# Sum of a state-space convolution and a gated linear unit: the first loads in halves, the transposes of the next blocks moved, and a new hand-written order of all steps

## The chip, the core and the metric

The kernel runs on one core of one Trainium2 chip. The metric is device time in microseconds (us) of one execution; three executions of the kernel before took 239.5, 239.64 and 239.75 us, so its median is 239.64 us. Lower is better. The engines are named as in the profile: PE is the matrix engine (TensorE; PEld are its weight loads), DVE the vector engine, ACT the scalar engine, POOL is GpSimd, and SP the sync engine, which only issues transfers (DMAs).

## What is computed

`x` is 2048 rows of 640, bf16. Its layernorm `xn` goes through two branches, and the result is the sum of both and of `x`:

```
xn = layernorm(x)                                  # x = A_q
k_shift = 4-tap causal filter of k along the rows  # taps shift_k, one set per column
kv  = k_shift * v
y   = causal convolution of kv with ssm_k along the rows (by FFT of 4096) + kv * ssm_D
A   = xn * y
B   = (sigmoid(xn @ w_gate) * (xn @ w_up)) @ w_down      # 640 -> 1728 -> 640
out = x + A + B
```

## The kernel before, in words

**Tiling.** The 2048 rows lie as 128 partitions times 16 blocks. The gated branch goes in four passes t = 0 to 3 of four blocks (512 rows) each; the convolution in five chunks c = 0 to 4 of 128 columns, each by a two-stage transform in matmuls whose intermediate results go out to DRAM and come back in another layout.

**The start** (L469 to L508). SP and ACT issue the loads of `x` blocks 0 to 3 and of the first columns of both weights (`load_w`, L171; `w[:, :, 0:256]` and `[256:512]`). PE runs 15 matmuls on a zeroed tile (`busy`), while DVE takes the layernorm of blocks 0 to 3 (`ln_stats`, `ln_aggr`, `ln_var`, `ln_xn`, with a power on POOL). For each block i of the first pass, `turn(i)` transposes `xn` on PE (`xn_mm`, L234) and copies the result on ACT (`xn_ev` through L223) to `xnT`; then four `quarter`s (L248) of five 128x128 matmuls each make the block's share of gate and up for the first two column groups fc = 0 and 1. In the kernel before, `turn(1)` stands behind the first two quarters of block 0, `turn(2)` and `turn(3)` behind the first and second pair of block 1.

**Everything else** is a list of steps, written to one program order per engine by a long string, `ORDER`. A letter takes the next step of its chain. Each engine works its own steps off in that order, and waits where data or a buffer is not there yet. The letters:

- `g`: a product of the gated branch on PE: a gate or up product of five 512-column matmuls (L257), at the end of a pass the one for the last 64 columns of both (`both_mm`, L278), or seven matmuls of the down projection (`down_mm`, L296).
- `s`: the sigmoid on ACT (L266, L284). `u`: the product with up on DVE (`up_ev` L272, `both_mul` L287), or the addition of the down result to `x` (L301).
- `k`: one of 16 DVE operations per chunk that make `kv` (`kv_op`, L329 to L338; the first of a chunk writes `acc` at L329). `H`, `D`: the turn of the filter on DVE (L315) and an addition on POOL. `t`, `Z`: the taps, on ACT or, for chunk 0, on POOL.
- `a`, `A`, `w`: first transform stage on PE (L355, L357), its copy on ACT, its write to DRAM (`wr1`, SP). `r`, `b`, `B`, `p`: read back (`rd2`, SP), second stage on PE (L388), copies on ACT, the two products on DVE (L401, L403). `c`, `C`, `W`: first inverse stage on PE (L417), copies on ACT, write to DRAM (`wr2`). `R`, `d`, `q`: read back (`rdb`), second inverse stage on PE (L456), and on DVE the product with `xn` (L461) and the addition to `x` (L466).
- `l`, `P`, `e`, `E`: layernorm on DVE and POOL, transposes on PE and copies on ACT for the passes 1 to 3.
- `m`, `n`, `h`, `K`, `V`, `T`, `o`: loads and stores, all issued by SP, in order.

**Buffers that tie the engines.** Products of the gated branch, transposes of passes 1 to 3 and `psb` share four PSUM tiles (`psG`, given out in rotation): the fifth tile needs the first one's reader to be done. For the last transpose of a pass (the fourth `e`), the tile needed is that of `both_mm`, which `both_mul` on DVE (L287) reads. The transform stages share two tiles (`psC`), read by ACT.

Of the kernel before, what the change touches and what calls it, by code (L numbers as in the profile page):

```python
# [19 lines left out]
P = 128  # L20
# [37 lines left out]
def kernel(  # L58
# [14 lines left out]
    nc = tc.nc  # L73
    xr = A_q.flatten_outer_dims().rearrange("(p b) d -> p b d", b=NB)
# [9 lines left out]
    S1d = nc.inline_tensor(s1bits, name="tabS1")  # L84
    TBd = nc.inline_tensor(tbbits, name="tabTB")
    SMd = nc.inline_tensor(smbits, name="tabSM")
# [11 lines left out]
    S1t = res.tile([P, NB, 2, P], U16, name="S1t")  # L98
    TBt = res.tile([P, 2, NB, P], U16, name="TBt")
    SMt = res.tile([P, 3, 32], U16, name="SMt")  # L100
# [4 lines left out]
    x = res.tile([P, NB, DM], BF16, name="x")  # L105
# [15 lines left out]
    sync = nc.sync  # L121
# [49 lines left out]
    def load_w(eng, lo, hi, u):  # L171
        if u == 0:
            eng.dma_start(w[:, :, lo:hi], wgr[:, :, lo:hi])
            return
        h = min(hi, 13 * P)
        eng.dma_start(w[:, :, UP + lo:UP + h], wur[:, :, lo:h])
        if hi == FF:
            eng.dma_start(w[:, :, FF:UP], wur[:, :, h:FF])
# [51 lines left out]
    def xn_mm(g, i):  # L230
        pool, tag = (psG, "g") if g else (psC, "c")
        xts[i] = pt = pool.tile([P, NC, P], BF16, name="pt", tag=tag)
        for c in range(NC):
            nc.tensor.transpose(pt[:, c, :], xn[:, 4 * g + i, c * P:(c + 1) * P], ident[:])  # L234

    def xn_ev(g, i, copy=act_copy):
        copy(out=xnT[:, i, :, :], in_=xts[i][:, :, :])
# [4 lines left out]
    def quarter(u, fc, i):  # L242

        if i == 0:
            pgs[u, fc] = psG.tile([P, 512], F32, name=("pg", "pu")[u], tag="g")
        o = u * UP + fc * P
        for c in range(NC):
            nc.tensor.matmul(pgs[u, fc][:, i * P:(i + 1) * P], lhsT=w[:, c, o:o + P], rhs=xnT[:, i, c, :],  # L248
                             start=(c == 0), stop=(c == NC - 1))
# [216 lines left out]
        nc.vector.tensor_tensor(xs, xs, chunks[c]["yx", m][:, :, :], ALU.add)  # L466


    sync.dma_start(x[:, 0, :], xr[:, 0, :])  # L469
    nc.scalar.dma_start(x[:, 1, :], xr[:, 1, :])  # L470
    nc.scalar.dma_start(x[:, 2:4, :], xr[:, 2:4, :])
    for u in range(2):
        load_w((sync, nc.scalar)[u], 0, 256, u)
    for u in range(2):
        load_w(sync, 256, 512, u)

# [7 lines left out]
    def turn(i):  # L484
        xn_mm(0, i)
        xn_ev(0, i)
# [13 lines left out]
    for i in range(4):  # L500
        for fc in range(2):
            for u in range(2):
                quarter(u, fc, i)
            if (i, fc) in ((0, 0), (1, 0), (1, 1)):
                turn(1 + i + fc)
    for fc in range(2):
        gate_ev(0, fc)
        up_ev(0, fc)  # L508
# [4 lines left out]
    def step(k, fn, *args):  # L513
        chains[k].append((fn, args))
# [16 lines left out]
    def hs(c):  # L531
        return [(load_h, c)]

    def ks(c):
        return [(load_halo, c), (load_k, c, 0, 8), (load_k, c, 8, NB)]

    def vs(c):
        return [(load_v, c, 0, 8), (load_v, c, 8, NB)]

    for k in ((load_w, sync, 512, 768, 0),  # L540
              (load_w, sync, 512, 768, 1),
              (load_taps, 0),
              (sync.dma_start, SMt[:], SMd.ap()),
              (load_w, sync, 768, 1024, 0),
              (load_w, sync, 768, 1024, 1),
              (load_w, sync, 1024, 1280, 0),
              (load_w, sync, 1024, 1280, 1),
              (load_wd, sync, 0, 7),
              *ks(0),
              (load_w, sync, 1280, FF, 0),  # L550
              (load_w, sync, 1280, FF, 1),
              *hs(0),
              *vs(0),
              (load_wd, sync, 7, NFC),
              (sync.dma_start, S1t[:], S1d.ap()),
              *hs(1),
              (load_x, sync, 1),
              *ks(1),
              *vs(1)):
        step("m", *k)  # L560
    for k in ((load_x, sync, 2), (load_x, sync, 3), (sync.dma_start, TBt[:], TBd.ap())):
        step("n", *k)
    step("Z", taps, 0)

# [54 lines left out]
        step("o", store, b, b + 1, 0, DM)  # L619

    ORDER = """
    mmmmmmmmmmZgmgsmgumgsmgugsgugsmgugskgkugkskgumkgsmkgumkgsmTguHgsHDgumgskkgukgskmgukgskgumkgkmgmutmkm
    auTaAHgAHDagAwlhauaAlglaglguwlgkPkgAulgAllleKeuKwEekaEekaEgkEVVHAgAHDgwughkgkugkskguKrrkaskaAgkAkguw
    gkskgutkgTskgkKuKaksaAKkgAkaugAwkaksaAkgkwakAgVuAVHasgwHDAauhgAkgkskwbugBrkgBkktbgpBrTkgBpsapsaAuguA
    apKgKswAkaugAkaKkwsakgVHAVgAuDHgswkcugCkgkskCgnuWakaAkgAkgukwbguBrlgBlgulbgBrlgBuglkPpgnulgllleenuEe
    kbEeprgEEgptkBgupBgkaauAgpAkapgswAkaugAkawksaAgkAkguwlcsglCgClbusgrlBWgBkugslpPkaauAgllAlglspwbgBruR
    kgBkscpguCpgCksWbkgBrugBkksbpgBrudBpdgsRqpcqgCqugCqpsWbgBrukgBspbgBrupdBadqsaApRgqAqapgwAqauseeEueaE
    egEEgAgAwaudAdqgwqRqcugCqgCguWbgBrgBugpbpdBrdqgBuqgqpcqgCupgCguWbgBrgBugpspRbgBrugBspcguCpgsCguWbsdr
    BdqgRBqqguqbpsgrBpgBugpspcgCugCsWbguBrdBgqspbqgBupgBspgucpsdCgRqRCqguWbsgBgBugpspgudsdqcqgCqoqdCudqg
    WqqgsqgugoguRRguggugguogodudqogqqogqdoudqogqqogqguogoouo  # L630
    """
    left = {k: iter(v) for k, v in chains.items()}
    for k in "".join(ORDER.split()):
# [33 lines left out]
```

## Time and profile before

| what | value |
|---|---|
| median of three executions | 239.64 us (239.5 to 239.75) |
| the profiled execution's own time | 239.41 us |
| its span, first to last instruction | 237.6 us |
| granted PE clock | 1.00 of full speed over the span |
| ACT busy | 141.2 us |
| HBM read, written | 36.12 MB, 18.35 MB |
| transfers, share of 16 DMA engines (hardware queue of SP) | 80.8% |
| down products, L296 | 448 matmuls, 64.3 us busy |
| gate and up products, L257 | 500 matmuls, 124.3 us busy |

The span is what the trace covers; 1.8 us of the profiled execution's time lie outside it. Durations below come from this one execution. A row such as "L257 ... x250 | 62.2, 379" gives the busy time of a group in us and the mean length of one instruction in ns; matmuls overlap, so the distance from one start to the next (the pitch) is shorter: five 512-column matmuls start 1.08 us before the next five. An "idle before" names what ended the wait.

### The profile page before, as it was taken

What the parts mean: (1) busy time and instruction counts of PE and PEld (TensorE: products, weight loads), DVE (VectorE), ACT (ScalarE), POOL (GpSimd) and SP (SyncE); (2) the same over time, 40 slices, a digit from 0 to 9 for tenths busy, and PEclk for the clock granted to TensorE, in tenths of its full rate; (3) what the DMA queues carried; (4) which work ended last, traced back from release to release, by engine and by line L of the source; (5) the groups of instructions that cost most, each with busy time, mean ns of one, the idle gap of its engine ahead of it and who ended that gap; (6) DMA issues with size and microseconds to landing.
All of it is one profiled execution on the core that took longest, in us unless ns stands there. A gap on an engine that the chain in (4) does not pass through costs nothing.

```text
span 237.6 us, 5553 instructions
## 1 busy us (share of the span) xinstructions
PE 231.4 (97%) x2265; PEld 135.1 (57%) x2265; DVE 190.3 (80%) x350; ACT 141.2 (59%) x178; POOL 11.2 (5%) x24
## 2 busy tenths in 40 slices
PE   8799999999999999999999999999999999999994
PEld 2564445878556455667754434577664434456782
DVE  3633889999999999999999999865585695968372
ACT  2342331728559897864888887997558858764000
POOL 4210000020000000002001000000000000000000
PEclk9999999999999999999999999999999999999999
DMA  7999999889998999999444888975939795285674
GB/s 212 292 314 233 259 322 298 183 249 284 253 311 243 253 295 297 284 267 319 148 183 152 234 230 258 227 228 203 241 109 222 186 281 123 89 238 144 196 237 134
DMA packets 88975, 54.82 MB, mean 231 GB/s; under 512 B 47670, under 2 KB 83062, under 8 KB 88694
## 3 DMA queue, kind: packets, MB, share of 16 engines
q1 hardware_dynamic: 88006, 53.66, 80.8%
q10 hardware_dynamic: 944, 0.82, 1.1%
q8 instruction: 17, 0.28, 0.5%
q14 instruction: 8, 0.07, 0.1%
HBM read 36.12 MB, written 18.35 MB: 229 GB/s over the span
## 4 chain that ended last, share of the span: by engine, by line
PE 95%; DMA 3%; ACT 0%; DVE 0%; ACTq 0%; issue 0%
PE pd L296 26%; PE pg L257 23%; PE pu L257 23%; PE psb L456 4%; PE ps L357 4%; PE ps L355 4%; PE ps L388 3%; DMA w<-in_B_w_up_dram 3%; PE psa L417 2%; PE pg L278 2%; PE pt L234 2%; PE pu L248 1%; PE pg L248 1%; ACT xnT L223 0%; DVE x L301 0%; ACT L119 0%
## 5 line engine op out<-in xcount | busy, mean ns | idle before, releaser
L257 PEld LDWEIGHTS <-w 128*128 128x128 bf16 x500 | 46.5, 98 | 54.3 <-issue 5.3
L296 PE MATMUL pd<-wd,hT 128*128 128x320 bf16 x448 | 64.3, 299 | 0.0
L257 PE MATMUL pg<-xnT,w 128*128 128x512 bf16 x250 | 62.2, 379 | 0.0
L257 PE MATMUL pu<-xnT,w 128*128 128x512 bf16 x250 | 62.1, 379 | 0.0
L296 PEld LDWEIGHTS <-hT 128*128 128x128 bf16 x448 | 42.8, 98 | 17.8 <-issue 1.7
L266 ACT ACTIVATE sig<-pg 128x512 bf16<-128x512 f32 x52 | 31.3, 605 | 30.1 <-PE pg L257 28.2
L272 DVE TENSOR_TENSOR hT<-sig,pu 128x512 bf16<-128x512 bf16 x52 | 35.2, 679 | 14.7 <-PE pu L257 9.3
L223 ACT CAST t<-ps 128x1024 bf16<-128x1024 f32 x40 | 39.1, 1023 | 11.4 <-DMA d<-t 6.3
L223 ACT CAST xz<-ps 128x1024 bf16<-128x1024 f32 x40 | 38.6, 1018 | 10.6 <-PE ps L388 10.5
L301 DVE TENSOR_TENSOR x<-pd,x 128x320 bf16<-128x320 f32 x32 | 15.4, 480 | 15.8 <-PE pd L296 15.7
L403 DVE TENSOR_TENSOR xz<-xz 128x2048 bf16<-128x2048 bf16 x20 | 24.4, 1220 | 0.2
L357 PE MATMUL ps<-kvh,S1t 128*128 128x128 bf16 x160 | 21.2, 219 | 0.0
L335 DVE TENSOR_TENSOR acc<-acc,tmp 128x1024 bf16<-128x1024 bf16 x30 | 20.7, 689 | 0.7
L355 PE MATMUL ps<-kvh,S1t 128*128 128x128 bf16 x160 | 21.2, 217 | 0.0
L333 DVE TENSOR_TENSOR tmp<-kx,sc 128x1024 bf16<-128x1024 bf16 x30 | 20.6, 687 | 0.4
L223 ACT CAST ao<-psa 128x1024 bf16<-128x1024 f32 x16 | 15.6, 1014 | 5.6 <-PE psa L417 3.5
L461 DVE TENSOR_TENSOR yx<-psb,xn 128x512 bf16<-128x512 f32 x20 | 13.8, 691 | 3.9 <-PE psb L456 2.9
L355 PEld LDWEIGHTS <-S1t 128*128 128x128 bf16 x160 | 15.5, 97 | 2.3
L357 PEld LDWEIGHTS <-S1t 128*128 128x128 bf16 x160 | 15.3, 96 | 2.3
L223 ACT COPY xnT<-pt 128x640 bf16<-128x640 bf16 x16 | 10.2, 709 | 10.8 <-PE pt L234 10.5
L198 DVE BATCH_NORM_STATS2 st<-x 128x6 f32<-128x320 bf16 x32 | 13.7, 471 | 2.8 <-DMA x<-in_A_q_dram 2.8
L401 DVE STREAM_SHUFFLE xz<-xz 128x512 f32<-128x512 f32 x20 | 14.6, 728 | 0.0
(44 smaller groups left out, 146.1 us busy)
## 6 DMA issues: line engine op xcount, KB each, us to landing
d<-t SPq DMA_DIRECT2D x20, 512.0 KB, 3.7
t<-d SPq DMA_DIRECT2D x20, 512.0 KB, 4.9
bi<-d SPq DMA_DIRECT2D x8, 512.0 KB, 5.5
d<-ao SPq DMA_DIRECT2D x6, 512.0 KB, 4.1
kx<-in_A_k_dram SPq DMA_DIRECT2D x10, 256.0 KB, 5.0
hn<-in_A_ssm_k_dram SPq DMA_DIRECT2D x20, 128.0 KB, 6.0
kvh<-in_A_v_dram SPq DMA_DIRECT2D x10, 256.0 KB, 5.2
x<-in_A_q_dram SPq DMA_DIRECT2D x3, 640.0 KB
```

The costliest lines, as they stand in the source:

```text
L223: nc.scalar.copy(out=out, in_=in_)
L257: nc.tensor.matmul(pg[:, :], lhsT=w[:, c, u * UP + fc * P:u * UP + (fc + 1) * P], rhs=xnT[:, :, c, :], start=(c == 0), stop=(c == NC - 1))
L266: nc.scalar.activation(sig[fc][:, :], pgs[0, fc][:, :], ACT.Sigmoid)
L272: nc.vector.tensor_tensor(hT[:, fc, :], sig[fc][:, :], pgs[1, fc][:, :], ALU.mult)
L296: nc.tensor.matmul(pd[:, :], lhsT=hT[:, fc, bb * P:(bb + 1) * P], rhs=wd[:, fc, 320 * half:320 * half + 320], start=(fc == 0), stop=(fc == ...
L301: nc.vector.tensor_tensor(x[:, 4 * t + bb, es], pds[bb, half][:, :], x[:, 4 * t + bb, es], ALU.add)
L333: nc.vector.tensor_tensor(d["tmp"][:, :, :], kx[:, lo + 3 - m:hi + 3 - m, :], sb(m), ALU.mult)
L335: nc.vector.tensor_tensor(d["acc"][:, :, :], d["acc"][:, :, :], d["tmp"][:, :, :], ALU.add)
L355: nc.tensor.matmul(ps[:, i, 0:P], lhsT=S1[:, b, h, :], rhs=cin[c]["kvh"][:, 0, b, :], start=True, stop=True)
L357: nc.tensor.matmul(ps[:, i, P:2 * P], lhsT=S1[:, b, h, :], rhs=hp[:, b // 2, b % 2, :], start=True, stop=True)
L401: nc.vector.stream_shuffle(z[:, 2, :, :].bitcast(F32), z[:, 1, :, :].bitcast(F32), swap)
L403: nc.vector.tensor_tensor(z[:, 1:3, :, :], z[:, 0:1, :, :].to_broadcast((P, 2, 8, P)), z[:, 1:3, :, :], ALU.mult)
```

## The change

**The first loads.** Blocks 0 and 1 of `x`, then columns 0 to 127 of both weights, then blocks 2 and 3 of `x` one by one, then columns 128 to 255: four transfers each for SP and ACT, in place of two for SP and three for ACT (SP goes on with columns 256 to 511, as before). **The turns.** `turn(i + 1)` stands behind the first gate quarter of block i. **The loads behind.** The taps, the small table `SMt`, the table `S1t`, half of `w_down` and the first blocks of `k` change places; so do the loads of the table `TBt` and the third part of `x`. **The order.** The whole string is new; the chains and the number of each letter are the same.

```diff
-    sync.dma_start(x[:, 0, :], xr[:, 0, :])
-    nc.scalar.dma_start(x[:, 1, :], xr[:, 1, :])
-    nc.scalar.dma_start(x[:, 2:4, :], xr[:, 2:4, :])
-    for u in range(2):
-        load_w((sync, nc.scalar)[u], 0, 256, u)
+    for n in range(2):
+        for i in range(2):
+            (sync, nc.scalar)[i].dma_start(x[:, 2 * n + i, :], xr[:, 2 * n + i, :])
+        for u in range(2):
+            load_w((sync, nc.scalar)[u], P * n, P * n + P, u)
     for u in range(2):
         load_w(sync, 256, 512, u)
...
         for fc in range(2):
             for u in range(2):
                 quarter(u, fc, i)
-            if (i, fc) in ((0, 0), (1, 0), (1, 1)):
-                turn(1 + i + fc)
+                if u + fc == 0 and i < 3:
+                    turn(i + 1)
...
     for k in ((load_w, sync, 512, 768, 0),
               (load_w, sync, 512, 768, 1),
-              (load_taps, 0),
-              (sync.dma_start, SMt[:], SMd.ap()),
               (load_w, sync, 768, 1024, 0),
               (load_w, sync, 768, 1024, 1),
+              (load_wd, sync, 0, 7),
+              *ks(0),
               (load_w, sync, 1024, 1280, 0),
               (load_w, sync, 1024, 1280, 1),
-              (load_wd, sync, 0, 7),
-              *ks(0),
+              (load_taps, 0),
               (load_w, sync, 1280, FF, 0),
               (load_w, sync, 1280, FF, 1),
               *hs(0),
               *vs(0),
               (load_wd, sync, 7, NFC),
-              (sync.dma_start, S1t[:], S1d.ap()),
               *hs(1),
               (load_x, sync, 1),
-              *ks(1),
-              *vs(1)):
+              (sync.dma_start, SMt[:], SMd.ap()),
+              (sync.dma_start, S1t[:], S1d.ap()),
+              *vs(1),
+              *ks(1)):
         step("m", *k)
-    for k in ((load_x, sync, 2), (load_x, sync, 3), (sync.dma_start, TBt[:], TBd.ap())):
+    for k in ((load_x, sync, 2), (sync.dma_start, TBt[:], TBd.ap()), (load_x, sync, 3)):
         step("n", *k)
...
     ORDER = """
-    mmmmmmmmmmZgmgsmgumgsmgugsgugsmgugskgkugkskgumkgsmkgumkgsmTguHgsHDgumgskkgukgskmgukgskgumkgkmgmutmkm
-    auTaAHgAHDagAwlhauaAlglaglguwlgkPkgAulgAllleKeuKwEekaEekaEgkEVVHAgAHDgwughkgkugkskguKrrkaskaAgkAkguw
-    gkskgutkgTskgkKuKaksaAKkgAkaugAwkaksaAkgkwakAgVuAVHasgwHDAauhgAkgkskwbugBrkgBkktbgpBrTkgBpsapsaAuguA
-    apKgKswAkaugAkaKkwsakgVHAVgAuDHgswkcugCkgkskCgnuWakaAkgAkgukwbguBrlgBlgulbgBrlgBuglkPpgnulgllleenuEe
-    kbEeprgEEgptkBgupBgkaauAgpAkapgswAkaugAkawksaAgkAkguwlcsglCgClbusgrlBWgBkugslpPkaauAgllAlglspwbgBruR
-    kgBkscpguCpgCksWbkgBrugBkksbpgBrudBpdgsRqpcqgCqugCqpsWbgBrukgBspbgBrupdBadqsaApRgqAqapgwAqauseeEueaE
-    egEEgAgAwaudAdqgwqRqcugCqgCguWbgBrgBugpbpdBrdqgBuqgqpcqgCupgCguWbgBrgBugpspRbgBrugBspcguCpgsCguWbsdr
-    BdqgRBqqguqbpsgrBpgBugpspcgCugCsWbguBrdBgqspbqgBupgBspgucpsdCgRqRCqguWbsgBgBugpspgudsdqcqgCqoqdCudqg
-    WqqgsqgugoguRRguggugguogodudqogqqogqdoudqogqqogqguogoouo
+    mmmmmmmmgmgsmgumgsgugsmgmugmsgugsgugZskgukgmskgmukmgskTgkugsHguDHgskmgukgskmgkmumgmksmmguHmgHDgmughu
+    kgkugkglgulaaAlgAlgwuglkPgtukTglnleleuEelaEkneaEkgEkAgkAakguAwkasknaAglwlaAgVuVAHgswHgDuhgslgulgskgu
+    rrlkgPskauaAlgllAlgkswkgukbsgKBkKrkgButbksgprBTkgBukaspaAgKkAaugKAkKwpasakAgpKwaugVHAVgsHDAguwkchskg
+    CkgCkubWskgBrkgBukaspeeEueaEkegEpEgAkglKAglKwbuguBrlgBlgublkPgBpKrkgtuBTlgllaluaAkgpAagAkwpaauAgkpwa
+    gAVHVgAuDHgwkcugCkkgCksbWkgBrukgBksapaAugkRAgpswbkgBrukgBkscpugCkdCpdgtRqsWkbqgBrqugBqksapaAgukAapds
+    waAqdgAkqqcwugCqkgCksWakaAugkAgkswkbugBrkRkgBksapaAugkAgpswbugBrkkgBksbpdBrudgqRBpasaAqgqApaqgwAupas
+    eeEueaEegEEdAgqAwqadAgqwqcugCgCugWbugBrgBgupbpgBrgBugpcpgCugCguWbgBrgBugpspRbgBrugBspcugCpgCsWbduBrd
+    qgRBqqgspqbugBrpgBspgucpsgCgCuWbsdBrdqgBqqguqbpsgRBpRgBugpspcguCgCsWbduBdqgBqqodsopdgqqoopgqgsqooucq
+    guCgCsWgugsguggRuRgugguggugdudqgqqogqdoudqgqqogqgouooguo
     """
```

More of the change, by code (lines that the diff above doesn't have):

```diff
@@ L621 @@
     ORDER = """
-    mmmmmmmmmmZgmgsmgumgsmgugsgugsmgugskgkugkskgumkgsmkgumkgsmTguHgsHDgumgskkgukgskmgukgskgumkgkmgmutmkm
-    auTaAHgAHDagAwlhauaAlglaglguwlgkPkgAulgAllleKeuKwEekaEekaEgkEVVHAgAHDgwughkgkugkskguKrrkaskaAgkAkguw
-    gkskgutkgTskgkKuKaksaAKkgAkaugAwkaksaAkgkwakAgVuAVHasgwHDAauhgAkgkskwbugBrkgBkktbgpBrTkgBpsapsaAuguA
-    apKgKswAkaugAkaKkwsakgVHAVgAuDHgswkcugCkgkskCgnuWakaAkgAkgukwbguBrlgBlgulbgBrlgBuglkPpgnulgllleenuEe
-    kbEeprgEEgptkBgupBgkaauAgpAkapgswAkaugAkawksaAgkAkguwlcsglCgClbusgrlBWgBkugslpPkaauAgllAlglspwbgBruR
-    kgBkscpguCpgCksWbkgBrugBkksbpgBrudBpdgsRqpcqgCqugCqpsWbgBrukgBspbgBrupdBadqsaApRgqAqapgwAqauseeEueaE
-    egEEgAgAwaudAdqgwqRqcugCqgCguWbgBrgBugpbpdBrdqgBuqgqpcqgCupgCguWbgBrgBugpspRbgBrugBspcguCpgsCguWbsdr
-    BdqgRBqqguqbpsgrBpgBugpspcgCugCsWbguBrdBgqspbqgBupgBspgucpsdCgRqRCqguWbsgBgBugpspgudsdqcqgCqoqdCudqg
-    WqqgsqgugoguRRguggugguogodudqogqqogqdoudqogqqogqguogoouo
+    mmmmmmmmgmgsmgumgsgugsmgmugmsgugsgugZskgukgmskgmukmgskTgkugsHguDHgskmgukgskmgkmumgmksmmguHmgHDgmughu
+    kgkgukglgulaaAlgAlgwuglkPgtukTglnleleuEelaEkneaEkgEkAgkAakguAwkasknaAglwlaAgVuVAHgswHgDuhgslgulgskgu
+    rrlkgPskauaAlgllAlgkswkgukbsgKBkKrkgButbksgprBTkgBukaspaAgKkAaugKAkKwpasakAgpKwaugVHAVgsHDAguwkchskg
+    CkgCkubWskgBrkgBukaspeeEueaEkegEpEgAkglKAglKwbuguBrlgBlgublkPgBpKrkgtuBTlgllaluaAkgpAagAkwpaauAgkpwa
+    gAVHVgAuDHgwkcugCkkgCksbWkgBrukgBksapaAugkRAgpswbkgBrukgBkscpugCkdCpdgtRqsWkbqgBrqugBqksapaAgukAapds
+    waAqdgAkqqcwugCqkgCksWakaAugkAgkswkbugBrkRkgBksapaAugkAgpswbugBrkkgBksbpdBrudgqRBpasaAqgqApaqgAwupas
+    eeEueaEegEEdAgqAwqadAgqwqcugCgCugWbugBrgBgupbpgBrgBugpcpgCugCguWbgBrgBugpspRbgBrugBspcugCpgCsWbduBrd
+    qgRBqqgspqbugBrpgBspgucpsgCgCuWbsdBrdqgBqqguqbpsgRBpRgBugpspcguCgCsWbduBdqgBqqodsopdgqqoopgqgsqooucq
+    guCgCsWgugsguggRuRgugguggugdudqgqqogqdoudqgqqogqgouooguo
     """
```

## Prediction

> **What bounds the kernel now.** The page first: two engines are nearly full.
>
> ```profile
> span 237.6 us, 5553 instructions
> PE 231.4 (97%) x2265; PEld 135.1 (57%) x2265; DVE 190.3 (80%) x350; ACT 141.2 (59%) x178; POOL 11.2 (5%) x24
> ```
>
> The chain that ended last, in order of time (start, length, what), shows where PE still loses time: only at the start.
>
> ```profile
> 1.65 7.12 DMA w<-in_B_w_up_dram
> 8.81 0.45 PE pu L248 x5
> 9.26 0.29 PE pt L234 x5
> 9.58 0.70 ACT xnT L223
> 10.32 0.44 PE pg L248 x5
> ...
> 14.21 0.28 PE pu L248 x5
> 14.49 1.09 PE pg L257 x5
> ```
>
> The first up quarter waits for its weights until 8.81; block 1's waits until 10.32 for its transposes, which stand behind it. From 10.32 to the last matmul at 234.36 I find no wait on PE in the trace.
>
> Third, busy time by stretch (stretch, length, then PE, PEld, DVE, ACT).
>
> ```profile
> 24.00:40.00 16.00, 16.00 (x78) 7.47 (x77) 14.40 (x22) 4.77 (x8) 0.42 (x1) 1.00 1.15 288
> 40.00:60.00 20.00, 20.00 (x197) 15.50 (x195) 19.63 (x41) 10.79 (x13) 2.17 (x3) 1.00 0.92 247
> ...
> 120.00:140.00 20.00, 20.00 (x217) 9.18 (x216) 19.57 (x41) 16.68 (x21) 1.01 (x1) 1.00 0.61 197
> 140.00:157.50 17.50, 17.50 (x206) 9.42 (x205) 16.43 (x29) 15.25 (x19) 0.00 (x0) 1.00 0.94 245
> 157.50:163.00 5.50, 5.50 (x70) 4.67 (x68) 1.56 (x3) 5.13 (x7) 0.00 (x0) 1.00 0.43 175
> ```
>
> DVE's 80% is an average: from 40 to 140 it is 98% busy, and has room only behind 158. So up to 158 there are two bounds. They meet where the timeline shows the last `both_mul` (L287) of pass 2 and the fourth transpose, which needs its PSUM tile:
>
> ```profile
> 23.24 0.69 DVE L272 TENSOR_TENSOR hT<-sig,pu 128x512 bf16<-128x512 bf16 x1 [1.47 <-PE pu L257]
> 23.85 0.68 DVE L329 TENSOR_TENSOR acc<-kx,sc 128x1024 bf16<-128x1024 bf16 x1
> ```
>
> ```profile
> 157.52 0.69 DVE L287 TENSOR_TENSOR hT<-sig,pg 64x512 bf16<-64x512 bf16 x1
> ...
> 158.40 0.44 PE L234 MATMUL pt<-ident,xn 128*128 128x128 bf16 x5
> ```
>
> L287 ends at 158.21, the transposes start at 158.40: a margin of 0.19 us, of which I count 0.13 as needed (weight load and signal). DVE's full stretch begins with the first `acc` at 23.85. Between 23.85 and 157.52, 133.67 us, the timeline shows waits of 0.27, 0.14, 0.14 and 0.87 (for up products, until 31.9), 0.13 and 0.81 (for ACT's copies): 2.36 us; 131.3 are work.
>
> **The change, part by part.**
>
> *Start on PE.* A group of five small matmuls has a pitch of 0.28; from the start of five transposes to the quarter that uses their copy it is 1.24 (6.54 to 7.78), or 1.22 where PE was warm. Now: first quarter at 7.78 as before, transposes of block 1 at 8.06 (their `xn` is written at 7.93), three quarters to 9.18, block 1 at 9.28; then 1.50 a block: 10.78, 12.28. Its four quarters end at 13.40, where before the first large product starts at 14.34: **0.94 us earlier**. `xn` of blocks 2 and 3 (9.38, 10.80) comes before its turns at 9.56 and 11.06.
>
> *Its transfers.* The packet records give 32 ns for a 512-byte packet of the first weights and 21 to 23 for the 256-byte packets of `kx` at 18 to 24 us. A load of 256 columns is 640 packets of 512 bytes, 40 to a DMA engine: 1.28 us; one of 128 columns 640 of 256: 0.84. So the four cost 3.36 against 2.56: all later loads move by 0.8. With 0.44 for each block of `x` (8 packets of 55 ns), from 2.3 us: first halves by 4.9, `x` by 5.7, second halves by 7.4; with the 0.5 to 1.0 us by which landings trail in this trace, 5.6, 6.5 and 8.2. Needed: 7.78; 6.71 for block 2 (its statistics); 8.62 and 8.90. All in time, by 0.2 to 0.7; late halves would cost up to the 0.94.
>
> The Trainium skill speaks against this: DMA: Bandwidth & Descriptors, section Specifications, wants 512 bytes or more per transfer for line rate, below it a read-modify-write. The row shows a milder price (21 ns for half the bytes of 32). By the rule a half would take as long as a whole, 1.28 us, and the time would be that of rival 4, 241.4; by the row it is the sum below.
>
> *Loads moved on SP.* Taps behind the weights 1024 to 1279: by queue order they land at 23.9, and 0.64 us of POOL copy (its row) ends at 24.7, under the first `k`. `S1t` behind `h` of chunk 1 and `x` blocks 4 to 7: packets before at 34 to 37, now some 5 us later, 43 to 44; the first `a` now comes at 46.7. The early `TBt` and `x` move 2.3 MB ahead of the chunk-0 writes. These cost nothing while PE work covers them; two covers become thin. Between `r` and its `b` for the first group PE has 18.6 us of listed work before and 5.2 now, while the first two such reads took 5.67 and 7.42 (I take 0 to 1.5 late). The first `K` of chunk 2 stands 2.6 us of listed PE work ahead of its first `k`; such loads took 5.0 (median), and only SP's running ahead hides them: 0 to 1 us of DVE wait.
>
> *The new order.* PE's work is the same, and its switches too: 20 `b` and 10 `c`, none adjacent, before and after. I therefore laid both strings out letter by letter with pitches from the trace (product 1.08, down half 0.95, `a` 0.45, `b` 0.48, `c` 0.69, `d` 0.45, `e` 0.28). The fourth `e` of pass 3 then stands at 144.1 us of PE work before and 145.0 now (two `d` more ahead of it): 158.40 both times, if PE never waits.
>
> DVE does not come along. Its first `acc` now stands behind five products, not four: up product 6 ends 0.94 earlier, so its `u` goes from 25.40 to 24.46, and `acc` to 25.07: **1.22 later than before**. Ahead of L287, the work is the same but for that one `u` (0.64), gone to the front, and four operations of `q` for chunk 1 that are new there (2 x 0.65 + 2 x 0.39 = 2.09): +1.45. Against this, dependent `k` operations back to back have a pitch of 0.72, separated ones 0.61; the new order separates more, and priced pair by pair the sum grows by only 0.73. I take the middle, 131.3 + 1.1 = 132.4. Waits: the early ones are 0.91 + 0.20 + 0.03 = 1.14 by PE's times; the late 0.94 of before is covered by DVE's lag. For read-backs, `K` and ACT's copies I add 0.5 (0 to 1.5). L287 then starts at 25.07 + 132.4 + 1.64 = 159.11, the transposes at 159.11 + 0.69 + 0.13 = 159.93, **1.53 later than 158.40**.
>
> *Behind it* 75.96 us of PE work followed (158.40 to 234.36); now two `d` fewer, 75.07. DVE has room again (1.56 busy of 5.5); write to read to `d` of the last chunk has 13.4 us against 11.7 needed before (213.55 to 225.29). Last matmul: 159.93 + 75.07 = 235.00, **0.64 later**; what follows it is unchanged. The profiled execution took 239.41, so 240.05; the median is 0.23 above it: **240.3 us**. Bounds: DVE work 132.0 and waits 1.14 give 0.25 less than before (239.4); 132.7 and 2.64 give 1.9 more (241.6).
>
> **Rivals.**
>
> 1. *DVE keeps up, the start's gain stays* (other side). PE leads if L287 starts by 157.6, that is if DVE needs 1.5 us less than 159.11: more separated pairs than I priced, and no new wait. For: the pair prices rest on few pairs, and DVE's lag makes its waits vanish. Against: `acc` starts later for certain. Then -0.94: 238.7.
> 2. *Loss and gain cancel*: DVE work and waits near the low bounds; 239.2 to 240.1, middle 239.6.
> 3. *A read-back stalls PE and DVE together*: first `b` 1.2 us or more late at 73 us, products and `u` move, and DVE, which bounds, loses it too: 240.3 + 1.2 = 241.5. For: 2.3 MB of early loads ahead. Against: `w` to `r` has 5.4 us of cover (4.2 before).
> 4. *The first halves come late*: at 1.28 each, the second halves land 1.76 later, near 10.0 against 8.90: the start 1.1 later, its gain gone, and `acc` 1.1 later too: 240.3 + 1.1 = 241.4. The row of 21 ns speaks against it. The rule of the Trainium skill quoted above (DMA: Bandwidth & Descriptors, Specifications) would bring this about.
>
> **How the numbers follow.** 0.2% is 0.48 us, about what a measurement of this kernel can tell from no change: faster is below 239.16, slower above 240.12. Chances: forecast 0.32, rival 1 0.22, rival 2 0.28, rival 3 0.13, rival 4 0.05. The forecast's own range, 239.7 to 241.0, lies to four fifths above 240.12, so slower is 0.26 + 0.13 + 0.05 and some of rival 2: 0.46. Faster 0.22; same 0.32. Range 238.6 to 241.9: it takes in rivals 1 to 4, and leaves out larger pile-ups behind DVE.
>
> **What would show it.** Right: first large product near 13.4; first `acc` near 25.1; DVE without waits from 40 to 158; a PE wait of 1 to 2 us at the last transposes of pass 3 near 159, released by DVE L287 or L272; no PE wait behind it. Wrong: no such wait (rival 1); a PE wait near 73 us at L388 behind a read-back, or DVE waiting for `kx` near 77 (rival 3); waits for weights before 13 us (rival 4). If PE waits for DVE much earlier, near 94 or 128, the DVE pitch was mis-sized.

## The result and the profile after

The changed kernel takes **243.72 us** (median of 6 runs, 243.0 to 244.54) where the kernel before took 239.68 on the same chip (239.5 to 239.77): ratio 1.0171, 95% interval 1.015 to 1.0193. It is slower, as forecast, but by 4.0 us where 0.6 was forecast, and outside the range. The profiled execution took 243.0, the shortest of the six. Ratios, here and below, leave out executions in a slower state (two of `af_all`, one of `af_taps`); medians are of all executions.

The page first, then its view of what PE waited for (what it waited for: us in all, times, longest).

```profile
span 241.2 us, 5547 instructions
PE 232.8 (97%) x2265; PEld 135.0 (56%) x2265; DVE 189.4 (79%) x350; ACT 140.5 (58%) x178; POOL 11.4 (5%) x24
```

```profile
PE pu L248 <- DMA w<-in_B_w_up_dram: 1.2, 1, 1.2
...
PE psa L417 <- ACT t L223: 1.0, 1, 1.0
PE ps L388 <- DMA t<-d: 0.5, 1, 0.5
```

The work is the same as before (2265 matmuls, 350 operations on DVE). Before, PE lost time only up to 10.32 us. Now it also stands at the first `b` (L388), the first `c` (L417) and twice at transposes behind L287. (The view counts from the modelled end of the matmul before; by the pitch of the matmuls the waits at `b` and `c` are 0.64 and 1.39 us; the waits at `a`, `b`, `c` and `d` below are by the pitch.) The chain that ended last shows where the start and the first `b` went (start, length, what):

```profile
0.72 3.38 DMA x<-in_A_q_dram
4.13 5.99 DMA w<-in_B_w_up_dram
10.17 0.45 PE pu L248 x5
...
58.46 4.94 DMA d<-t
...
65.45 4.14 DMA d<-t
69.65 5.33 DMA t<-d
...
75.12 0.44 PE ps L388 x16
```

Block 1 of `x` stands ahead of the second half of the up weights: that load is issued only at 4.13, because it waits for the semaphore that the load issued at 0.72 had taken. It lands at 10.12, and block 0's second up quarter starts at 10.17. Further on the chain is write, write, read-back, and then `b`.

What DVE waited for between 23 and 163 us, in the same form:

```profile
...
DVE acc L329 <- DMA kx<-in_A_k_dram: 1.2, 1, 1.2
DVE hT L272 <- ACT sig L266: 1.2, 1, 1.2
DVE acc L329 <- POOL sc L149: 0.7, 1, 0.7
DVE kvh L315 <- DMA hn<-in_A_ssm_k_dram: 0.4, 1, 0.4
```

The timeline shows the two ends of DVE's full stretch (start, length, engine, line, operation; idle time before it and its releaser in brackets):

```profile
26.36 0.64 POOL L149 COPY sc<-sraw 128x512 bf16<-128x512 bf16 x1 [16.15 <-DMA sraw<-in_A_shift_k_dram]
27.04 0.69 DVE L329 TENSOR_TENSOR acc<-kx,sc 128x1024 bf16<-128x1024 bf16 x1 [0.71 <-POOL sc L149]
...
161.71 0.69 DVE L287 TENSOR_TENSOR hT<-sig,pg 64x512 bf16<-64x512 bf16 x1
162.45 0.44 PE L234 MATMUL pt<-ident,xn 128*128 128x128 bf16 x5
```

The first `acc` waits for the taps and starts at 27.04 (before 23.85). The last `both_mul` of pass 2 starts at 161.71 (before 157.52), and the transposes behind it at 162.45 (before 158.40). The first large product starts at 14.58 (before 14.34), the last matmul ends at 237.52 (before 234.36).

Last, the stretches in which the new order loads early (stretch, length, PE, PEld, DVE, ACT, POOL, clock, DMA share, GB/s), first before, then after:

```profile
52.00:56.00 4.00, 4.00 (x53) 3.43 (x52) 3.93 (x10) 3.75 (x6) 0.36 (x1) 1.00 0.94 262
56.00:60.00 4.00, 4.00 (x30) 2.65 (x28) 3.97 (x7) 2.49 (x3) 0.42 (x1) 1.00 1.06 308
60.00:64.00 4.00, 4.00 (x32) 2.35 (x31) 3.90 (x8) 2.05 (x4) 0.00 (x0) 1.00 0.89 262
```

```profile
52.00:56.00 4.00, 4.00 (x52) 3.23 (x50) 4.00 (x10) 1.88 (x4) 1.09 (x1) 1.00 1.09 286
56.00:60.00 4.00, 4.00 (x40) 2.91 (x39) 3.86 (x7) 3.98 (x7) 0.00 (x0) 1.00 0.98 397
60.00:64.00 4.00, 4.00 (x30) 2.19 (x28) 3.93 (x10) 1.47 (x3) 0.12 (x1) 1.00 1.00 347
```

The DMA engines are full in both, but 4.1 MB move here (4 us times 286, 397 and 347 GB/s) where 3.3 MB moved; `TBt` and the third and fourth group of `x` are among them. In the trace, writes of `d` issued near 84 and 86 us land after 4.75 and 4.79 us; the two near 72 and 75 in the kernel before took 2.96 and 3.00.

### The profile page after: what moved, and what is told of

The parts are those of the page before. It is cut to its first block, busy times and chain, and to the rows that moved or that the text cites. A ratio compares the mean times of both kernels' runs of the same rounds, so it can differ in the third digit from the quotient of the medians.

```text
span 241.2 us, 5547 instructions
## 1 busy us (share of the span) xinstructions
PE 232.8 (97%) x2265; PEld 135.0 (56%) x2265; DVE 189.4 (79%) x350; ACT 140.5 (58%) x178; POOL 11.4 (5%) x24
## 4 chain that ended last, share of the span: by engine, by line
PE 68%; DVE 16%; DMA 10%; issue 3%; ACT 0%; DVEq 0%; ACTq 0%; SPq 0%
PE pd L296 26%; PE pg L257 14%; PE pu L257 14%; DVE hT L272 4%; DMA d<-t 4%; PE psb L456 3%; PE ps L388 2%; DMA w<-in_B_w_up_dram 2%; DVE tmp L333 2%; DVE acc L335 2%; DVE xz L403 2%; DMA t<-d 2%; PE psa L417 2%; PE ps L357 2%; PE ps L355 1%
## 5 line engine op out<-in xcount | busy, mean ns | idle before, releaser
L266 ACT ACTIVATE sig<-pg 128x512 bf16<-128x512 f32 x52 | 31.3, 605 | 26.4 <-PE pg L257 24.7
```

Source lines behind the costliest of these rows:

```text
L266: nc.scalar.activation(sig[fc][:, :], pgs[0, fc][:, :], ACT.Sigmoid)
```

## The experiments

In all tables "acc" is the start of the first `acc`, "L287" that of the last `both_mul` of pass 2, ahead of the transposes of pass 3 (the expectations call it the L287 of pass 3), both from the profiled execution, which can lie 1 to 2 us from the median (`af_taps` 244.52, `af_k` 244.78); ratios are to the kernel before, run on the same chip.

### The start and the order, each alone

`start_alone` is the kernel before with the first loads and turns of the change; `order_alone` is the changed kernel with the first loads and turns of before. In `start_fixed` and `after_fixed` (the changed kernel) SP issues the second half of the up weights:

```
-            load_w((sync, nc.scalar)[u], P * n, P * n + P, u)
+            load_w((sync, sync if n else nc.scalar)[u], P * n, P * n + P, u)
```

> Only the first loads and the turns are new; load lists and step order are those of before. Theory A (the second half of the up weights is issued late, because its load waits for a DMA semaphore, and the start's gain is lost there): an up quarter of block 0 waits until about 10.2 us, the first large product starts near 14.6 instead of 13.4, and the time is 239.7 to 240.2. Rival B (the start is right by itself and only the order's traffic spoils it): first large product near 13.4, 238.7 to 239.2.

> As start_alone, but the second half of the up weights is issued by SP, ahead of columns 256 to 511, where no semaphore is in use yet. Theory A: it lands near 8 us, no weight wait after 9 us, first large product near 13.4. What that is worth has two answers. A1 (DVE sets the end of pass 3): the first acc can't start before its K at about 23.5, so DVE gains at most 0.3 us, PE waits 0.6 to 0.8 us at the last transposes near 157.5, and the time is 239.3 to 239.6. A2 (PE sets it): all of the 0.94 stays, 238.7. If the semaphore isn't the cause, the first large product stays near 14.6 and the time near that of start_alone.

> Load lists and step order of the changed kernel with the first loads and turns of before: first large product at 14.34. Theory A1 (DVE sets the end of pass 3, and its first acc waits for the taps, which now come behind the weights 1024 to 1279): acc at 26.2 to 26.5, last L287 of pass 3 near 161, time 242.0 to 243.0, most of the loss. Theory A2 (PE's own waits at the first b near 75 us and the first c near 91 us are the loss, each added to PE): about the changed kernel less 0.24, 243.4. Rival C (order and start only hurt together): 239.7 to 240.5.

> The changed kernel with the second half of the up weights issued by SP ahead of columns 256 to 511. Theory A1 (DVE sets the end of pass 3): the first large product comes 1.2 us earlier, near 13.4, but the first acc still waits for the taps near 27.0, so the L287 of pass 3 stays near 161.5 and PE waits there for 1 us or more: 243.2 to 243.8, no gain. Theory A2 (PE's lost time adds up): 242.4 to 242.7.

| run | median us | ratio, 95% interval | first large product | acc | L287 |
|---|---|---|---|---|---|
| before | 239.59 | | 14.34 | 23.85 | 157.52 |
| start_alone | 240.27 | 1.0021, 1.0001 to 1.0041 | 14.38 | 23.88 | 158.64 |
| start_fixed | 240.54 | 1.0028, 1.0005 to 1.005 | 13.46 | 23.41 | 157.79 |
| order_alone | 243.16 | 1.0163, 1.0116 to 1.0209 | 14.54 | 26.20 | 162.25 |
| after_fixed | 243.96 | 1.0167, 1.0127 to 1.0207 | 14.22 | 26.96 | 163.87 |

The cause at the start is settled: in `start_alone` the quarter waits until 9.96, in `start_fixed` the second half lands at 7.80, no weight wait is left, and the first large product starts 0.88 us earlier than before the change. The edit takes away the wait for the semaphore and the place behind SP's other loads together; what each cost is not separated. (In `after_fixed` it comes at 14.22 because the warm-up matmuls ran at half their rate for longer, 3.41 us instead of 2.64; no weight wait there either.) But nothing of the 0.88 reaches the end. Step by step against the kernel before, `start_fixed` keeps it until `e` near 54 us, where 0.45 goes to DVE's late `xn`, and loses 0.57 more at an `a` near 77, where ACT's copy is late. DVE had lost its lead at the first `h_turn` of chunk 1 (43.71 against 43.98), which waits 0.53 for its load. The time, 240.54, missed A1 (239.3 to 239.6) and A2 (238.7), and PE doesn't wait at the last transposes of pass 3, where A1 put the loss. `after_fixed` (243.96) gains nothing either. The order with its load lists holds nearly all of the loss.

### Single waits mended

All on `after_fixed`. `af_taps` moves `(load_taps, 0)` back behind the weights 512 to 767. `af_k` moves the `K` steps, `af_tab` the step of `TBt` (and swaps it with the last group of `x` in the list); `af_all` makes all three edits.

```
af_k:   -gDuhgsl  -sgKBkKrkgBu  -AgKkAaugKAkKwpasakAgpKwaugVHAVgsHDAguwkch
        +gDuKKKhgsl  +sgBkrkgBu  +AgkAaugAkwpasakAgpwaugVHAVgsHDAguwKKKkch
af_tab: -wkasknaAglw  -ubWskgBrkgBukasp
        +wkaskaAglw   +ubWnskgBrkgBukasp
```

> The changed kernel with the mended start (after_fixed) and the taps loaded behind the weights 512 to 767 again, as before the change. The first acc then waits for its up product and K alone: about 25.0 to 25.3 us, 1.7 earlier than in after_fixed. Theory A1 (DVE sets the end of pass 3 by itself): the last L287 of pass 3 comes 1.2 to 1.7 earlier and the time is 242.2 to 242.8. Theory A2 (PE's own waits at the first b near 75 us and at the first c near 91 set it): those stay, and the time is that of after_fixed within 0.4. Theory B (both chains have lost about the same, so neither mended alone gives anything): as A2, and only af_all gains.

> after_fixed with the loads of K for chunk 2 ahead of h for chunk 3, near 66 us, and those of chunk 3 behind the writes of chunk 1. The 1.2 us that DVE waits for K near 80 us go, and the writes near 84 to 86 us have fewer loads ahead of them, so they take nearer the 3.0 us of before than 4.8, and the 1.4 us wait of the first c near 91 shrinks to 0.3 or less. Theory A1: 1.2 earlier, 242.6 to 242.9. Theory A2: 1 to 1.4 earlier, 242.5 to 243. Theory B: acc is still late, gain under 0.5, 243.5 or more.

> after_fixed with the 1 MB of TBt loaded behind the first W (near 95 us) instead of near 52, and the third x group in its place. Theory T (traffic of early loads makes writes and read-backs late): writes of chunk 0 at 50 to 61 us take 1 us or more less than 5 to 6, ACT's wait for them (2.5 us near 61) goes, the first b near 75 doesn't wait; the time falls by 0.5 to 1.0, to 243 to 243.5. Theory B: DVE, late by acc and K, hides it, no gain.

> after_fixed with all three edits: taps early, K of chunk 2 early and of chunk 3 behind the writes, TBt late. Theory B and A1: first acc near 25.2, no DVE wait for K, no PE wait at 75 and at most 0.3 at 91, last L287 of pass 3 near 159.0 and the time 240.2 to 241.0, what was forecast for the change. Theory A2: about the sum of af_k and af_tab, 241.5 to 242. Rival R (the order itself is at fault, DVE needs more time for its work in it): no better than 242.5.

| run | median us | ratio, 95% interval | acc | L287 | acc to L287 |
|---|---|---|---|---|---|
| after (profile) | 243.72 | 1.0171, 1.015 to 1.0193 | 27.04 | 161.71 | 134.67 |
| af_taps | 243.15 | 1.0139, 1.0103 to 1.0175 | 25.17 | 163.19 | 138.02 |
| af_k | 246.99 | 1.0286, 1.0249 to 1.0323 | 26.54 | 163.77 | 137.23 |
| af_tab | 242.14 | 1.0116, 1.008 to 1.0151 | 26.50 | 160.66 | 134.16 |
| af_all | 245.64 | 1.0217, 1.018 to 1.0254 | 24.87 | 163.62 | 138.75 |

(`af_tab` is shown without the swap in the list.) Each edit took away the wait it was aimed at, and another load or read-back came late in its place. `af_taps` starts `acc` 1.8 us earlier and then has a new PE wait of 1.1 us at the first `a`, for `S1t` at 47.98, and one of 1.2 at the first `b`. `af_k` has no wait for `K` any more, but its loads go ahead of the first read-back, and `b` waits 3.6 us until 78.04. `af_all` waits 1.9 there and 2.5 at a later `b`, near 108, behind a read-back that SP issued 4 us after `TBt` at its new place and that landed after 7.3 us. Taking 1 MB out of the stretch from 52 to 60 gave the lowest ratio (`af_tab`: writes near 59 and 73 land after 2.67 and 3.07 us, one near 63 after 5.38; no wait at the first `b`, none above 0.3 for `K`), but its interval overlaps that of `after_fixed` (1.0127 to 1.0207). `af_all`, expected at 240.2 to 241.0, fell by its time to its rival R, that the order itself is at fault; the runs with fewer loads, below, test that.

### The early loads, late again and alone

`af_late` puts the last group of `x` behind the fourth write of chunk 1 and `TBt` behind the third of chunk 2; `af_late_c` also moves the first `c`. `before_tab` does the reverse: the kernel before, with only these two loads at 52 us. `af_tab_w` is `af_tab` with `K` and `V` of chunk 3 behind the fourth write. For `af_late` and `af_late_c` only the new places are shown; the two `n` leave their old ones, and the list is x 2, x 3, `TBt`.

```
af_late:    -HDAguwkch   -kpwagAVHV
            +HDAguwnkch  +kpwnagAVHV
af_late_c:  -chskgCkgCkubWskgB
            +hskgckgCkusCkgbWB
before_tab: -laglguwlgk... n, n later    (list: x 2, x 3, TBt)
            +laglguwnnlgk...             (list: x 3, TBt, x 2)
af_tab_w:   -AgKkAaugKAkKwpasakAgpKwaugVHAVgsHDAguwkch
            +AgKkAaugAkwpasakAgpwaugHAgsHDAguwKKKVVkch
```

> The changed kernel with the mended start, and both early loads put back: the last x group behind the fourth write of chunk 1 (near 91 us), TBt behind the third write of chunk 2 (near 112). Theory T (these 1.7 MB, which the changed order loads at 52 to 60 us, make writes, read-backs and K late): writes at 58 to 66 us take 4 us or less instead of 5 to 5.5, no PE wait at the first b near 75, no DVE wait for K near 80, the time at or below that of af_tab (242.1): 241.0 to 242.0. Rival: what af_tab gained was the 1 MB alone, 242.0 to 242.5; or the loads only hurt at their new places (a wait at another b), 242.5 or more.

> af_late with the first c one product later and its second copy behind another product, so that PE works where it waits 0.9 to 1.4 us near 90. If PE's own waits count (A2): 0.9 to 1.4 less than af_late, and no stretch at half clock behind it. If DVE sets the end of pass 3 (A1): the wait moves to the transposes of pass 2 or 3 (near 97 and 160), and the time is that of af_late within 0.4.

> The kernel before with the last x group and TBt loaded at 52 us, as the changed order does it; nothing else. If the early traffic is enough by itself to do harm: a read-back or K is late between 60 and 95 us and the time is 240.5 to 242. If it harms only where the order leaves little PE work between a read-back and its b (18.6 us before, 5.2 after): 239.5 to 240.1, no PE wait at a b, write latencies longer by 1 us or more.

> af_tab with the K and V loads for chunk 3 behind the fourth write of chunk 1, so that three writes have no load issued shortly ahead of them. Theory T: those writes take 3.5 us or less instead of 4.8, ACT's copies come 1 us earlier, the wait of the first c near 90 shrinks from 0.9 to 0.3 or less, and the time is 241.0 to 241.8 (af_tab 242.1). If DVE's chain is already the later one there: wait gone, time as af_tab, with more wait at the transposes near 161.

| run | median us | ratio, 95% interval | acc | L287 |
|---|---|---|---|---|
| af_late | 242.88 | 1.0128, 1.009 to 1.0166 | 26.14 | 161.93 |
| af_late_c | 243.60 | 1.0139, 1.0101 to 1.0176 | 26.55 | 162.85 |
| before_tab | 243.24 | 1.0135, 1.0111 to 1.0159 | 24.35 | 160.49 |
| af_tab_w | 248.44 | 1.0355, 1.0325 to 1.0385 | 26.92 | 167.70 |

`before_tab` is the telling one. In the old order, with nothing else changed, these 1.7 MB at 52 us cost 1.35%, some 3.2 us, more than either answer had. (In the profiled execution PE lost 0.50 at the start, where the up weights landed later than in the trace of before and which the edit doesn't touch, and 1.68 and 0.83 at the two `a` shown.) The 18.6 us of work between read-back and `b` do cover the read-backs, so the second answer was right on that, and wrong on the time: the harm comes another way. The timeline of `before_tab`, ACT and PE:

```profile
74.83 1.01 ACT L223 CAST t<-ps 128x1024 bf16<-128x1024 f32 x1 [1.98 <-DMA d<-t]
75.89 0.22 PE L355 MATMUL ps<-kvh,S1t 128*128 128x128 bf16 x1 [1.52 <-ACT t L223]
78.72 1.93 ACT L223 CAST t<-ps 128x1024 bf16<-128x1024 f32 x2 [1.47 <-DMA d<-t]
79.78 0.22 PE L355 MATMUL ps<-kvh,S1t 128*128 128x128 bf16 x1 [0.67 <-ACT t L223]
```

ACT's copy needs a `t1` buffer (there are two), and that is free only when its write has landed. Writes from 49 to 60 us take 6.3, 7.6 and 5.1 us here (before: 5.0 and 3.6 for those that the trace shows), later ones are issued later (SP took 2.8 us to issue a read-back at 65.90, and the write behind it went out at 68.79), ACT's copy is late, and PE's next `a` has no PSUM tile. The wait of the first `c` at 91 us in the changed kernel is the same thing: its second tile is free when ACT's last copy ends, at 91.02, and ACT took up these copies at 88.60, just after the write issued at 83.75 had landed (88.50). So is DVE's wait for `sig` near 65: ACT made it behind a copy that had waited 2.53 us for a write, until 63.49.

`af_late` has no wait at the first `b` and none for `K`, but 1.4 us for `hn` of chunk 1, 1.2 at `c` and 0.9 near 131 at the first `d`, for a read-back issued at 126.10. Its ratio is lower than that of `after_fixed` (1.0128 against 1.0167), but the intervals overlap, and it is not below `af_tab`. Theory T had expected 241.0 to 242.0. In `af_late_c` the wait at `c` is 0.81, and 0.57 and 0.50 stand at the `b` and the transposes behind it, nearly as A1 had it; the time is no better. `af_tab_w` went wrong: a `b` near 110 waits 3.9 us for a read-back.

### With fewer loads in both orders

If traffic is the rest of the loss, the same order must cost little where it is lighter. `before_light2` and `af_light2` (`after_fixed` with the taps early) leave the same loads out: `K` of chunks 2 to 4 isn't loaded, and columns of the weights stand in for both tables, so that 32.2 MB are read instead of 36.1:

```
     def load_k(c, lo, hi):
+        if c > 1:
+            return
...
-    S1 = S1t.bitcast(BF16)
-    TB = TBt.bitcast(BF16)
+    flat = w.rearrange("p c f -> p (c f)")
+    S1 = flat[:, 0:4096].rearrange("p (b h q) -> p b h q", b=NB, h=2)
+    TB = flat[:, 4096:8192].rearrange("p (h b q) -> p h b q", b=NB, h=2)
```

> The kernel before with some 3.5 MB of loads left out and nothing in their place: columns of the weights stand in for both tables, and K of chunks 2, 3 and 4 isn't loaded (the data of chunks 0 and 1 is used again). The base for af_light2. Theory T (the old order has its loads covered): 238.6 to 239.6, as before or little less, since DVE's first acc and work stay and only the wait for hn or the writes can go. If its loads held it back: 238.5 or less.

> The changed order with the mended start and the taps early, with the same loads left out and the same weights standing in as in before_light2. Theory T: no PE wait above 0.4 at the first b or c, last L287 of pass 3 near 159.0, and the time 0.2 to 1.2 above before_light2. Rival O (the order itself): 2.5 or more above it.

| run | median us | ratio, 95% interval | first large product | acc | L287 |
|---|---|---|---|---|---|
| before_light2 | 239.82 | 1.0021, 1.0002 to 1.004 | 14.08 | 23.59 | 157.20 |
| af_light2 | 240.89 | 1.0071, 1.0041 to 1.0101 | 13.14 | 24.80 | 159.19 |

The two orders now differ by 1.1 us. With all loads and the same start and taps (`af_taps`) it was 3.3 (ratio 1.0139). Two lines of `af_light2`'s timeline (L332 and L290 are the L329 and L287 of the other kernels), and what PE waited for there:

```profile
24.80 0.68 DVE L332 TENSOR_TENSOR acc<-kx,sc 128x1024 bf16<-128x1024 bf16 x1
...
159.19 0.69 DVE L290 TENSOR_TENSOR hT<-sig,pg 64x512 bf16<-64x512 bf16 x1
```

```profile
PE ps L391 <- ACT sig L269: 0.7, 1, 0.7
...
PE pt L237 <- DVE hT L290: 0.3, 1, 0.3
```

`acc` at 24.80 and L290 at 159.19 are the forecast's 25.07 and 159.11; the wait at `c` is nearly gone (0.35 by the pitch). One wait that the expectation excluded (none above 0.4) stays, 0.82 at the first `b`. The profile names ACT's `sig`, which `b` doesn't read; likelier is the read-back, issued at 69.69 behind a write that took 7.06 us (issued at 62.54, landed at 69.60), whose own landing the trace doesn't show. So the traffic's part isn't wholly gone here. The old order gains nothing from the lighter traffic, so its loads were covered.

An earlier pair set the tables to zero on POOL instead:

> The kernel before with some 3.5 MB of loads left out: both tables are set to zero by POOL near 12 us instead of loaded, and K of chunks 2, 3 and 4 isn't loaded (the data of chunks 0 and 1 is used again). It is the base for af_light. Theory T (the old order has its loads covered): 239.0 to 239.8, no gain of more than 0.6, since DVE's first acc and its work stay. If the loads held it back too: 238.5 or less.

> The changed order with the mended start and the taps early, and the same loads left out as in before_light. Theory T (the order is at fault only through loads, writes and read-backs that come late): first acc near 25.2, no PE wait above 0.3 at the first b or c, last L287 of pass 3 near 159.0, and the time 0.2 to 1.2 above before_light, what was forecast for the change. Rival O (DVE and ACT can't follow this order even with light traffic): 2.5 or more above before_light, with the waits at 91 us and at the transposes still there.

It gave 246.74 (ratio 1.0303, 1.0282 to 1.0324) and 247.38 (1.0325, 1.0305 to 1.0345). In both DVE stood still for 6.6 us near 10 us because of the memsets (last section) and PE waited 5.3 and 5.6, which gave the loads a head start; the orders differ by 0.64.

### The turns alone, and loads behind writes in the old order

`turns_only` is the kernel before with the turns alone; `turns_w` also moves `K` and `V` loads behind the next write at six places of the old order.

> The kernel before with the changed turns alone. Without halves the up weights still land at 8.8: PE's quarters and turns give the first large product near 13.8 instead of 14.34 (first quarter 7.78, block 0 to 9.65 with its wait, then 1.4 to 1.5 a block). By A1 DVE can't follow, since its first acc waits for K at 23.3 and its first h op for chunk 1 waits for a load: 239.3 to 239.7, no difference to be measured. By A2 the 0.5 stays: 239.1.

> The kernel before with the changed turns and, in the order of before, K and V loads moved behind the next write. Theory T: the waits at the first products of chunks 0 and 2 (near 54 and 77 us, 0.5 to 0.6 each in turns_only) go, since writes land 1 us earlier, and some of the 0.6 that the turns win at the start stays: 238.9 to 239.4. If DVE's chain holds it: as turns_only, 239.4 to 239.7; if a K or V comes too late, above 240.

`turns_only` took 239.54 (ratio 0.9987, 0.9969 to 1.0006): first large product at 13.72, L287 at 158.27, no gain that can be measured. `turns_w` took 242.63 (1.0118, 1.01 to 1.0135): a wait of 1.27 at an `a` near 75 stayed, and DVE waited 1.15 for the third group of `x` near 107; in the profiled execution another 1.2 went to a wait for the first up weights (0.4 in `turns_only`), which the moved loads don't touch. No version here beats the kernel before.

## Why the prediction was right and wrong

**The start: wrong.** The step that failed is "All in time, by 0.2 to 0.7": the second half of the up weights was put at 8.2 and landed at 10.12. Its issue was taken to follow the load ahead of it; it waits for a semaphore until 4.13, and then its packets move (8.0 to 9.4) behind those of the columns 256 to 511, which SP had issued before it. First large product 14.58 instead of 13.40. With the load on SP, 13.46: the rest of that sum was right.

**The taps: mis-sized.** Forecast to land at 23.9, copy done at 24.7, "under the first `k`"; they landed at 26.31, the copy ended at 27.00, and `acc` waited 0.71 for it. With the 1.18 us of the late start, `acc` came 1.97 later than forecast (27.04 against 25.07).

**DVE sets the end of pass 2: right, and close in size partly by luck.** From `acc` to L287 the forecast had 132.4 + 1.64 = 134.04 us; it took 134.67 there, 134.39 in `af_light2`. In the profile of after that sum is made of other terms: the gaps on DVE add up to about 3.0 us, not 1.64, and the work to 131.6, not 132.4. With `acc`, that makes L287 161.71 instead of 159.11. Behind it the 75.07 us of PE work came out exactly (162.45 to 237.52), and the tail took 0.4 more than assumed. So the sum's 2.95 us over the forecast (243.0 against 240.05) are 1.97 at `acc`, 0.63 in DVE's stretch and 0.4 in the tail, less 0.1 between L287 and the transposes.

**"For read-backs, `K` and ACT's copies I add 0.5 (0 to 1.5)": the step that failed most.** In the profile of after DVE waited 1.23 for ACT's `sig` near 65, 1.24 for `K` near 80 and 0.43 for `hn`, 2.9 in all, and PE 0.64 at the first `b` and 1.39 at the first `c`, which the forecast didn't see. Mending `acc` didn't bring its 1.97 back: in `af_taps`, with `acc` at 25.17 as forecast, the stretch to L287 took 138.02, 4.0 more than the forecast's 134.04. The two bounds lost about the same, so PE waited only 0.22 at the last transposes of pass 3 where 1 to 2 was announced, and mending one chain gives little. The runs put a size on it: the order with the mended start and the taps early loses 3.3 us with all loads and 1.1 with fewer. The forecast for the order alone, +0.64, was near the 1.1; some 2.2 are traffic, by this pair, give or take about 1 by the intervals. The sentence "These cost nothing while PE work covers them" looked for the cover at the read-backs. The thin cover was at `t1`, whose write must land before ACT goes on.

**Rivals.** 1 and 2 fell. 3 had the right cause ("2.3 MB of early loads ahead") and one of the places (75 us), and stopped at one wait. 4 gave the start's loss (near 10.0, measured 10.12) by luck, and not by the price of small packets: it was the order of issue. In the first 6 us 256-byte packets took 18 ns, and from 6 to 12 us 512-byte ones 34. (In the first 6 us of the kernel before, 512-byte packets took 29.) The rule quoted from the Trainium skill (DMA: Bandwidth & Descriptors, Specifications) asks for 512 bytes or more for line rate; that a half costs as much as a whole was the prediction's estimate from it. Here 256-byte packets cost more per byte, 18 ns against half of 29, but not as much as a whole, and the measurement decides.

What stays open: how the 2.2 us divide between the waits, and what of the other 0.7 (4.0 less 3.3) the start and the taps cost; the intervals overlap there. The variants differ by 1 to 2 us and more from run to run of one kernel, and each edit shifted loads that others needed.

## What to carry to other kernels

Where the DMA engines are full, a load moved earlier is paid for by whatever is issued behind it: list what it overtakes (writes whose buffers must come free, read-backs, the next chunk's inputs), and look for the thinnest cover among them, not for the one named in the change. An early start on one engine lasts only until that engine meets something that did not come earlier too (here DVE's `xn`, and ACT's copies behind writes). And check when a load can be issued, not only where it stands in the code.

## What the runs showed of the hardware

**Half clock behind a wait.** In the profile of `after_fixed` the first `c` waited 0.79 and 1.39 us (by the pitch of its matmuls); then the granted clock fell (third figure from the end):

```profile
92.00:93.00 1.00, 1.00 (x33) 0.34 (x4) 0.93 (x3) 0.73 (x2) 0.00 (x0) 0.77 0.58 226
93.00:94.00 1.00, 1.00 (x4) 0.34 (x3) 0.97 (x2) 1.00 (x2) 0.00 (x0) 0.50 0.94 314
...
95.00:96.00 1.00, 1.00 (x4) 0.30 (x2) 0.96 (x3) 0.00 (x0) 0.00 (x0) 0.53 0.75 205
```

Products ran at 427 ns a matmul instead of 213 until near 96, some 1.7 us lost (8 matmuls at 214 ns more). The profile of after, with 1.39 alone, has no such stretch. Of six runs of `af_k` two had a mean clock of 1.000 and took 244.78 and 246.07, four had 0.993 and took 246.96 to 247.57. The profiled execution was one of the two: it had waited 3.6 us at a `b` and its clock stayed at 1.00, while in `af_tab_w` 3.9 us at a `b` was followed by 3.4 us at half clock (110.6 to 114.1). So a wait can cost twice, in some executions; that this is part of the spread of the other variants is likely, but their slower executions have no trace. The Trainium skill (TensorE: Matmul & The Clock Gate, section HAM oscillation — how this bites in real kernels) names idle gaps above about 3.4 us; here 2.2 us in two pieces were enough in this execution of `after_fixed`, and 3.6 us were not in that of `af_k`.

**POOL holds DVE.** In `before_light` one DVE operation that takes 0.45 us elsewhere lasted as long as two memsets on POOL (timelines of POOL and DVE):

```profile
10.01 3.52 POOL L516 MEMSET S1t<- 128x4096 bf16 x1
10.10 7.06 DVE L223 TENSOR_SCALAR xn<-x,mv,rstd 128x640 bf16<-128x640 bf16 x1 [0.67 <-POOL rstd L218]
...
13.45 3.52 POOL L516 MEMSET TBt<- 128x4096 bf16 x1
```

It agrees with the Trainium skill (SBUF — State Buffer, section SBUF: two separate sides): the port pair that the two share is an exclusive lock for a whole instruction. Here it was held for two.
